# A fused attention and expert kernel: the attention tile's TensorE work regrouped into scores, values and transposes

## The chip, the cores and the metric

The kernel runs on one core of a Trainium2 chip. The metric is the device time of one execution in microseconds (us); the kernel before takes 827.62 us (median of three runs, 827.51 to 828.70). TensorE is called PE in the rows, its weight loads PEld, VectorE DVE, ScalarE ACT, GpSimd POOL, SyncE SP.

## The reference

Local attention with a few global keys, then four experts with fixed shares, then a gated product:

```
scores = scale * q @ k.T  - slope[h] * dist         # 2 batches, 8 heads, 768 positions, 64 wide
keep   = key < 8  or  0 <= q_pos - k_pos < 96       # all else is masked
a      = exp(scores - max);  a = a / (sum(a) + 1e-9)
x      = (a @ v)                                    # 1536 tokens x 512
out    = sum_e p[:, e] * (relu(x @ w1[e]) @ w2[e])  # 4 experts, 512 -> 1024 -> 512
final  = (((out @ wa) * (out @ wb)) @ w3) @ w_out
```

## The kernel before

The attention stage takes the first tenth of the time. It goes over twelve tiles of 128 queries. The first tile of each batch has only its own 128 keys; the ten others see a window of 232 keys (96 before, 8 global, 128 own). A tile has eight heads in two groups of four.

For a tile the work runs through five engines:

- TensorE: `scores` (line 246, eight matmuls into four PSUM tiles `sp`), `transposes` of the weights (line 284, four PSUM tiles `tp`, two for each group of heads; each holds two heads, and I call it a quarter of the tile), `values` (lines 325 and 326, into the PSUM tile `op`).
- VectorE: `least` for each head (line 261: bias, and the running minimum that becomes the exponent's offset), `inverse_sums` for each group (lines 231 and 232), the copy of one `tp` of each group to SBUF (line 291), and the low part of x, `xl` (line 468).
- ScalarE: `weights` for each head (line 272: the exponential with its sum; I number them 1 to 8 in a tile), the copy of the other `tp` of each group (line 291), the high part of x, `xh` (line 462), and from the seventh tile on a cast of a piece of an expert weight (line 343).
- GpSimd: `normalize` for each head (line 300), and the low part of the weight piece (line 344).

A later stage reads x as a high and a low part, hence two passes over each `op`.

The order on every engine is written out by hand: the loop over tiles (from line 357) emits the calls, and each engine executes its own in that order. An engine that waits for one instruction holds up all that stand behind it. Each loop step works on three tiles at once: scores of its own tile `u`, transposes of the tile one back, values of the tiles one and two back. TensorE's order in a step is: scores of u; transposes of group 0 of one back; values of group 1 of two back and of group 0 of one back; transposes of group 1 of one back. So four groups of matmuls follow each other in a step. PSUM has eight banks, four for `sp`, two for `tp` (`ps_t`), two for `op` (`ps_o`).

At the head of a step VectorE has the high cast of half an `op` and one copy, then two `least`; `inverse_sums` of the tile before comes after those. After the loop come the last tile's remaining steps, mixed with three expert products that are taken ahead (`experts.up_ahead`, lines 56 to 58); then the experts and the gate fill the rest, with matmuls of 128x512 almost without a gap.

Of the kernel before, what the change touches and what calls it, by code (L numbers as in the profile page):

```python
# [8 lines left out]
F32 = mybir.dt.float32  # L9
# [7 lines left out]
PSUM = bass.MemoryType.PSUM  # L17

P = 128
# [5 lines left out]
WIN = LW + GW + P  # L25
N, DM, E, F = B * S, H * D, 4, 1024
NPAIR = H // 2
KC, FC = DM // P, F // P
# [89 lines left out]
def banded_attention(tc, g, x_hi, x_lo, slots, experts):  # L118
    nc = tc.nc
    with ExitStack() as ctx:  # L120
# [5 lines left out]


        ps_s = ctx.enter_context(tc.tile_pool(name="ps_s", bufs=4, space=PSUM))
        ps_t = ctx.enter_context(tc.tile_pool(name="ps_t", bufs=2, space=PSUM))
        ps_o = ctx.enter_context(tc.tile_pool(name="ps_o", bufs=2, space=PSUM))  # L130
        mk = ctx.enter_context(tc.tile_pool(name="mk", bufs=1))
        two = ctx.enter_context(tc.tile_pool(name="at2", bufs=2))
        three_ = ctx.enter_context(tc.tile_pool(name="at3", bufs=3))
# [89 lines left out]
        later_bias(nc.gpsimd, (0, 1))  # L223

        st = {}
        raws, banks, firsts = [], [], {(order[-2], 1), (order[-1], 1)}

        def inverse_sums(u, gr):
            hs = slice(4 * gr, 4 * gr + 4)
            r, sums = st[u]["r"][:, hs], st[u]["sums"][:, hs]  # L230
            nc.vector.scalar_tensor_tensor(r, sums, 1e-9, sums, op0=ALU.add, op1=ALU.max)
            nc.vector.reciprocal(r, r)  # L232
# [21 lines left out]
        def least(u, gr, hh):  # L254

            w = WIN if u % NQ else P
            h = 4 * gr + hh
            t = three_.tile([P, WIN], F32, name="t", bufs=4)
            bb = bias[:, h] if u % NQ else bias0[:, h]
            nm = g.negmax[:, u * H + h : u * H + h + 1]  # L260
            nc.vector.tensor_tensor_reduce(  # L261
                out=t[:, 0:w], in0=st[u]["sp", gr][hh % 2][:, hh // 2, 0:w], in1=bb, scale=-SCALE,
                scalar=3.0e38, op0=ALU.add, op1=ALU.min, accum_out=nm,
            )
            st[u]["t", h] = t, nm

        def weights(u, gr, hh):

            w = WIN if u % NQ else P
            h = 4 * gr + hh  # L270
            t, nm = st[u].pop(("t", h))
            nc.scalar.activation(  # L272
                st[u][gr][:, hh, 0:w], t[:, 0:w], AF.Exp, bias=nm, scale=-1.0, accum_out=st[u]["sums"][:, h : h + 1]
            )

        def transposes(u, gr):
            pt = st[u][gr]
            tps = []
            for half in range(2):
                tp = ps_t.tile([P, 2, 2, P], F32, name="tp")  # L280
                for hh in range(2):
                    for j in range(2 if u % NQ else 1):
                        c = slice(j * (LW + GW), j * (LW + GW) + P)
                        nc.tensor.transpose(tp[:, hh, j], pt[:, 2 * half + hh, c], g.ident)  # L284
                tps.append(tp)
            st[u][gr] = tps

        def copy(u, gr, half):
            nj = 2 if u % NQ else 1
            sb = two.tile([P, 2, 2, P], F32, name="ptT", bufs=4)  # L290
            (nc.scalar.copy if half else nc.vector.tensor_copy)(sb[:, :, 0:nj], st[u][gr][half][:, :, 0:nj])
            st[u][gr][half] = sb
# [17 lines left out]
        def values(u, gr):  # L310

            i = u % NQ
            va, vo = values_of[u]
            if (u, gr) in firsts:
                banks.append((ps_o.tile([P, 4, P], F32, name="op"), []))
            o = banks[-1][0][:, 2 * len(banks[-1][1]) :][:, 0:2]
            banks[-1][1].append((u, gr))
            st[u]["o", gr] = o
            for hh in range(4):
                h, ab = 4 * gr + hh, hh % 2  # L320
                sb = st[u][gr][hh // 2]
                os_ = o[ab * D : (ab + 1) * D, hh // 2]
                vs = slice(h * D, (h + 1) * D)
                if i:
                    nc.tensor.matmul(os_, va[:, vs], sb[0 : LW + GW, ab, 0], start=True, stop=False)  # L325
                    nc.tensor.matmul(os_, vo[:, vs], sb[:, ab, 1], start=False, stop=True)  # L326
                else:
                    nc.tensor.matmul(os_, vo[:, vs], sb[:, ab, 0], start=True, stop=True)

        def outputs(u, gr):  # L330
            return st[u]["o", gr], x_hi, x_lo, u, slice(2 * gr, 2 * gr + 2)


        def load_weight(f):

# [7 lines left out]
            nc.scalar.copy(hi, raw)  # L343
            return lambda: nc.gpsimd.tensor_tensor(lo, raw, hi.bitcast(F32), op=ALU.subtract)

        def high(steps, copy=None):
            for step in steps:
                split_x_hi(nc, *outputs(*step), copy)

        def low(steps):  # L350
            for step in steps:
                split_x_lo(nc, *outputs(*step))

        nt = len(order)
        first = second = []
        for m, u in enumerate(order):
            one_back, two_back = (order[m - k] if m >= k else None for k in (1, 2))
            if 0 <= m - W_TILE < 4:
                load_weight(m - W_TILE)
            if m + 2 < nt:  # L360
                fetch(order[m + 2])
            if m + 1 < nt:
                fetch_v(order[m + 1])
            scores(u, 0)
            scores(u, 1)
            if m < len(FILL):
                keep_warm(FILL[m])
            high(second, nc.vector.tensor_copy)
            if m >= 2:
                for half in range(2):  # L370
                    copy(two_back, 1, half)
            n = m - W_TILE - 2
            rest = piece(n // 2, n % 2 * 256, n % 2 * 256 + 256) if n >= 0 else None
            for hh in range(2):
                least(u, 0, hh)
                weights(u, 0, hh)
            if m:
                inverse_sums(one_back, 1)
                transposes(one_back, 0)
                copy(one_back, 0, 1)  # L380
            least(u, 0, 2)
            weights(u, 0, 2)
            if m == 0:
                first_bias(1)
            least(u, 1, 0)
            least(u, 0, 3)
            weights(u, 0, 3)
            weights(u, 1, 0)
            if m:
                copy(one_back, 0, 0)  # L390
                normalize(one_back, 1, range(4))
            if m == 1:
                later_bias(nc.scalar, (5,))
            least(u, 1, 1)
            weights(u, 1, 1)
            inverse_sums(u, 0)
            least(u, 1, 2)
            weights(u, 1, 2)
            gone = first, second
            first, second = [(two_back, 1)] if m >= 2 else [], [(one_back, 0)] if m else []  # L400
            firsts.update((first + second)[0:1])
            for step in first + second:
                values(*step)
            high(first)
            low(gone[0])
            least(u, 1, 3)
            weights(u, 1, 3)
            low(gone[1])
            if m == 0:
                later_bias(nc.vector, (2, 3))  # L410
            if m == 1:
                later_bias(nc.scalar, (6, 7))
                later_bias(nc.vector, (4,))
            normalize(u, 0, range(4))
            if rest:
                rest()
            if m:
                transposes(one_back, 1)
        last, prior = order[-1], order[-2]
        out = experts.up_ahead(ps_s)  # L420
        for half in range(2):
            copy(prior, 1, half)
        high(second)
        inverse_sums(last, 1)
        normalize(last, 1, range(3))
        normalize_last(last, 1)
        transposes(last, 0)
        for half in range(2):
            copy(last, 0, half)
        low(first + second)  # L430
        values(prior, 1)
        out()
        high([(prior, 1)])
        low([(prior, 1)])
        transposes(last, 1)
        for half in range(2):
            copy(last, 1, half)
        out = experts.up_ahead(ps_s)
        for f in range(3):
            piece(f, F // 2, F)()  # L440
        values(last, 0)
        values(last, 1)
        out()
        out = experts.up_ahead(ps_s)
        high([(last, 0), (last, 1)])
        low([(last, 0), (last, 1)])
        split(nc, *slots[3], raws[3])
        out()

# [10 lines left out]
def split_x_hi(nc, tp, x_hi, x_lo, u, ks, copy=None):  # L460
    c, j = divmod(u, TPC)
    (copy or nc.scalar.copy)(x_hi[c][:, ks, j * P : (j + 1) * P], tp)


def split_x_lo(nc, tp, x_hi, x_lo, u, ks):
    c, j = divmod(u, TPC)
    sl = slice(j * P, (j + 1) * P)
    nc.vector.tensor_tensor(x_lo[c][:, ks, sl], tp, x_hi[c][:, ks, sl].bitcast(F32), op=ALU.subtract)
# [847 lines left out]
```

## Time and profile before

| | us |
|---|---|
| median of three runs | 827.62 |
| the profiled execution | 827.62 |
| its span on the chip | 825.7 |
| TensorE busy | 814.3 |
| VectorE busy | 509.9 |
| GpSimd busy | 315.6 |
| ScalarE busy | 283.5 |

The time outside the span is 1.9 us. A row of the timeline has the start, the duration, the engine and line, what is written and read, how many instructions the row merges, and in brackets how long the engine was idle before and what it waited for. The matmul rows of scores, transposes and values count two passes for each 4-byte matmul of scores and values. A step from the start of one row to the start of the next on the same engine is the time that the engine really gives to the first; durations overlap a little.

### The profile page before, as it was taken

The numbers are of one execution on the slowest core, as the hardware profiler recorded it, in microseconds if no ns is written. First come the engines' busy times: TensorE is split into PE (matmuls) and PEld (weight loads), VectorE is DVE, ScalarE is ACT, GpSimd is POOL, SyncE is SP. The second block draws the span as 40 slices with busy tenths as digits, with TensorE's granted clock in tenths as the row PEclk, the third lists the DMA queues.
The fourth block names the chain that finished last, engine by engine and source line by source line (L and its number), as shares of the span: only waits on it lengthen the run. The fifth ranks groups of instructions, "written<-read, shape, count | busy, mean of one in ns | idle before, by whom it ended". The sixth has DMA issues, their size and how long they took to land.

```text
span 825.7 us, 11047 instructions
## 1 busy us (share of the span) xinstructions
PE 814.3 (99%) x4003; PEld 669.5 (81%) x4003; DVE 509.9 (62%) x967; ACT 283.5 (34%) x595; POOL 315.6 (38%) x318
## 2 busy tenths in 40 slices
PE   8999999999999999999999999999999999999997
PEld 5888888888888888888888888888788888888875
DVE  7997446557755557778648573665543743887850
ACT  6997221223321213333324321332542432333210
POOL 6787023534356554641243341422370003333300
PEclk9999999999999999999999999999999999999999
DMA  8950333558453547743101102111523210201011
GB/s 252 274 152 2 104 129 119 154 161 250 158 166 107 152 150 231 228 153 102 39 25 52 39 26 64 52 64 43 189 88 101 78 52 26 102 26 52 0 52 55
DMA packets 38133, 88.11 MB, mean 107 GB/s; under 512 B 3690, under 2 KB 9882, under 8 KB 38070
## 3 DMA queue, kind: packets, MB, share of 16 engines
q1 hardware_dynamic: 37398, 86.79, 33.2%
q8 instruction: 33, 0.54, 0.3%
q10 hardware_dynamic: 672, 0.54, 0.3%
q14 instruction: 30, 0.25, 0.1%
HBM read 73.66 MB, written 13.66 MB: 106 GB/s over the span
## 4 chain that ended last, share of the span: by engine, by line
PE 96%; DVE 1%; ACT 1%; DMA 1%; issue 0%; DVEq 0%; ACTq 0%
PE z L56 18%; PE z L58 18%; PE z L57 18%; PE o L58 11%; PE o L56 11%; PE o L57 11%; PE tp L284 2%; PE sp L246 2%; PE op L325 2%; PE op L326 1%; ACT pt L272 1%; DMA keys<-in_k_dram 1%; PE sp L56 0%; PE sp L58 0%; PE sp L57 0%
## 5 line engine op out<-in xcount | busy, mean ns | idle before, releaser
L58 PE MATMUL z<-xh,sl 128*128 128x512 f32 x428 | 166.6, 389 | 0.0
L56 PE MATMUL z<-xh,sh 128*128 128x512 f32 x428 | 166.5, 389 | 0.0
L57 PE MATMUL z<-xl,sh 128*128 128x512 f32 x428 | 166.5, 389 | 0.0
L565 POOL TENSOR_TENSOR cr<-cr,cb 128x512 f32<-128x512 f32 x40 | 51.6, 1290 | 126.6 <-issue 118.8
L58 PEld LDWEIGHTS z<-xh,sl 128*128 128x128 f32 x428 | 80.3, 188 | 17.0 <-DVE sl L51 0.2
L57 PEld LDWEIGHTS z<-xl,sh 128*128 128x128 f32 x428 | 80.4, 188 | 16.8
L56 PEld LDWEIGHTS z<-xh,sh 128*128 128x128 f32 x428 | 80.3, 188 | 16.5
L51 POOL TENSOR_TENSOR sl<-wr,sh 128x512 fp32r<-128x512 f32 (+1 forms) x32 | 32.1, 1023 | 149.5 <-ACT sh L50 149.5
L51 DVE TENSOR_TENSOR sl<-wr,sh 128x1024 fp32r<-128x1024 f32 (+1 forms) x57 | 70.4, 1241 | 23.5 <-ACT sh L50 22.8
L819 POOL TENSOR_TENSOR acc<-acc,t 128x512 f32<-128x512 f32 x36 | 49.2, 1399 | 84.8 <-DVE t L818 84.8
L50 ACT CAST sh<-wr 128x1024 fp32r<-128x1024 f32 (+2 forms) x89 | 70.5, 815 | 21.4 <-PE z L57 10.3
L550 POOL TENSOR_SCALAR ca<-ca 128x512 f32<-128x512 f32 x40 | 61.8, 1545 | 26.8 <-ACT ca L548 26.8
L718 DVE TENSOR_TENSOR t<-t,z 128x512 f32<-128x512 f32 x56 | 37.4, 680 | 31.9 <-PE z L58 27.4
L300 POOL TENSOR_TENSOR pt<-pt,r 128x232 f32<-128x232 f32 (+1 forms) x95 | 48.8, 545 | 14.6 <-DVE r L232 5.2
L56 PE MATMUL z<-sh,sh 128*128 128x512 f32 x128 | 49.9, 390 | 0.8 <-DVE t L818 0.8
L58 PE MATMUL z<-sh,sl 128*128 128x512 f32 x128 | 49.8, 389 | 0.0
L57 PE MATMUL z<-sl,sh 128*128 128x512 f32 x128 | 49.8, 389 | 0.0
L272 ACT ACTIVATE pt<-t,negmax 128x232 f32<-128x232 f32 (+1 forms) x96 | 44.5, 466 | 7.3 <-DVE negmax L261 7.1
L51 POOL TENSOR_TENSOR sl<-t,sh 128x256 fp32r<-128x256 f32 (+1 forms) x24 | 23.0, 973 | 31.2 <-ACT sh L50 31.0
L261 DVE CUSTOM_DVE_ANT_0 t<-sp,bias 128x232 f32<-128x232 f32 (+1 forms) x96 | 32.4, 368 | 0.8 <-PE sp L246 0.8
L56 PE MATMUL o<-h0h,sh 128*128 128x512 f32 x84 | 32.8, 390 | 0.0
L57 PE MATMUL o<-h0l,sh 128*128 128x512 f32 x84 | 32.7, 389 | 0.0
(256 smaller groups left out, 1733.9 us busy)
## 6 DMA issues: line engine op xcount, KB each, us to landing
wr<-in_w_moe_dram SPq DMA_DIRECT2D x44, 512.0 KB, 3.4
raw<-in_w3t_dram SPq DMA_DIRECT2D x16, 512.0 KB, 4.1
raw<-in_w_ab_dram SPq DMA_DIRECT2D x16, 512.0 KB, 4.4
wr<-wab_d SPq DMA_DIRECT2D x16, 512.0 KB, 3.2
raw<-in_w_out_dram SPq DMA_DIRECT2D x8, 512.0 KB, 3.4
w3t_d<-cr SPq DMA_DIRECT2D x16, 256.0 KB, 2.5
wab_d<-cr SPq DMA_DIRECT2D x16, 256.0 KB, 2.2
wr<-w3t_d SPq DMA_DIRECT2D x8, 512.0 KB, 3.3
```

Of the source, the lines that this page charges most:

```text
L50: nc.scalar.copy(hi, src)
L51: (lo_engine or nc.vector).tensor_tensor(lo, src, hi.bitcast(F32), op=ALU.subtract)
L56: nc.tensor.matmul(out, wh, xh, start=start, stop=False)
L57: nc.tensor.matmul(out, wh, xl, start=False, stop=False)
L58: nc.tensor.matmul(out, wl, xh, start=False, stop=stop)
L261: nc.vector.tensor_tensor_reduce(out=t[:, 0:w], in0=st[u]["sp", gr][hh % 2][:, hh // 2, 0:w], in1=bb, scale=-SCALE, scalar=3.0e38, op0=ALU ...
L272: nc.scalar.activation(st[u][gr][:, hh, 0:w], t[:, 0:w], AF.Exp, bias=nm, scale=-1.0, accum_out=st[u]["sums"][:, h : h + 1])
L300: nc.gpsimd.tensor_tensor(pt[:, hh, 0:w], pt[:, hh, 0:w], r[:, hh : hh + 1].to_broadcast([P, w]), op=ALU.mult)
L550: nc.gpsimd.tensor_scalar(a, a, 2.0**-15, None, op0=ALU.max)
L565: nc.gpsimd.tensor_tensor(rest, rest, top.bitcast(F32), op=ALU.add)
L718: add = lambda o, a, b: nc.vector.tensor_tensor(o, a, b, op=ALU.add)
L819: nc.gpsimd.tensor_tensor(acc[c][:, d], acc[c][:, d], t, op=ALU.add)
```

## The change

In each loop step TensorE now does three groups: scores of both head groups of `u`, values of both head groups of the tile two back, transposes of both head groups of the tile one back. A tile's `op` is written in one go into one bank (`ps_o` has one buffer), `ps_t` gets three buffers, and `t`, the tile between `least` and `weights`, six in place of four. The x casts go over the whole `op` (128x512): high on ScalarE, low on VectorE; the high cast of half an `op` on VectorE is gone. `inverse_sums` and `normalize` of the tile before's second group move to the head of the step.

```diff
-        ps_t = ctx.enter_context(tc.tile_pool(name="ps_t", bufs=2, space=PSUM))
-        ps_o = ctx.enter_context(tc.tile_pool(name="ps_o", bufs=2, space=PSUM))
+        ps_t = ctx.enter_context(tc.tile_pool(name="ps_t", bufs=3, space=PSUM))
+        ps_o = ctx.enter_context(tc.tile_pool(name="ps_o", bufs=1, space=PSUM))
...
-            high(second, nc.vector.tensor_copy)
+            if m:
+                inverse_sums(one_back, 1)
+                normalize(one_back, 1, range(4))
             if m >= 2:
                 for half in range(2):
                     copy(two_back, 1, half)
...
-            for hh in range(2):
+            for hh in range(4):
                 least(u, 0, hh)
                 weights(u, 0, hh)
-            if m:
-                inverse_sums(one_back, 1)
-                transposes(one_back, 0)
-                copy(one_back, 0, 1)
...
             least(u, 1, 1)
+            least(u, 1, 2)
+            inverse_sums(u, 0)
+            if m >= 2:
+                values(two_back, 0)
+                values(two_back, 1)
+                split_x_hi(nc, *outputs(two_back))
             weights(u, 1, 1)
-            inverse_sums(u, 0)
-            least(u, 1, 2)
+            if m:
+                transposes(one_back, 0)
+                for half in (1, 0):
+                    copy(one_back, 0, half)
             weights(u, 1, 2)
-            for step in first + second:
-                values(*step)
-            high(first)
-            low(gone[0])
             least(u, 1, 3)
             weights(u, 1, 3)
-            low(gone[1])
+            if m >= 2:
+                split_x_lo(nc, *outputs(two_back))
...
             if m:
                 transposes(one_back, 1)
...
+        for gr in range(2):
+            values(prior, gr)
         out()
+        for gr in range(2):
+            transposes(last, gr)
```

VectorE at the head of a loop step, before: `xh` is the high part of x, `ptT` the transposed weights, `t` and `negmax` come from `least`, `r` and `sums` belong to the tile before.

```order
L462 CAST xh0_70<-op_586 128x2x128 [waits Activation_49]
L291 COPY ptT_649<-tp_613 128x512 [waits PE_49]
L261 ISA t_653,negmax_69<-sp_632,bias_97 128x232 [waits PE_49]
L261 ISA negmax_69 128x1
L261 ISA t_656,negmax_69<-sp_633,bias_97 128x232 [waits PE_49]
L261 ISA negmax_69 128x1
L231 SCALAR_TENSOR_TENSOR r_529<-sums_528 128x4 [waits Activation_49]
L232 RECIPROCAL r_529<-r_529 128x4 [waits DVE_49]
```

VectorE at the same place after the change:

```order
L449 TENSOR_TENSOR xl0_73<-op_557,xh0_70 128x4x128 [waits Activation_49]
L231 SCALAR_TENSOR_TENSOR r_517<-sums_516 128x4 [waits Activation_49]
L232 RECIPROCAL r_517<-r_517 128x4 [waits DVE_49]
L291 COPY ptT_640<-tp_599 128x512 [waits PE_49]
L261 ISA t_644,negmax_69<-sp_618,bias_97 128x232 [waits PE_49]
L261 ISA negmax_69 128x1
```

The row that waits for ScalarE's sums of the tile before stood behind a cast, a copy and two `least`; now it stands in front of the copy and of all `least`.

ScalarE over one loop step late in the stage, before:

```order
L291 COPY ptT<-tp 128x512
L343 CAST sh_80<-wr 128x256
L272 ACTIVATE pt,sums<-t,negmax 128x232 x2
L291 COPY ptT<-tp 128x512
L272 ACTIVATE pt,sums<-t,negmax 128x232 x5
L462 CAST xh_72<-op 128x2x128
L272 ACTIVATE pt,sums<-t,negmax 128x232
```

ScalarE over the same step after the change:

```order
L291 COPY ptT<-tp 128x512
L340 CAST sh_80<-wr 128x256
L272 ACTIVATE pt,sums<-t,negmax 128x232 x5
L443 CAST xh_72<-op 128x4x128
L272 ACTIVATE pt,sums<-t,negmax 128x232
L291 COPY ptT<-tp 128x512
L272 ACTIVATE pt,sums<-t,negmax 128x232 x2
```

The copy of the first group's `tp` moved from behind exponential 2 to behind exponential 6; the cast covers 512 columns in place of 256 and stands behind exponential 5 in place of 7.

TensorE, the second half of the transposes and the next tile's scores after the change:

```order
L284 MATMUL tp_599<-ident_63,pt_425 128x128 [waits Pool_49]
L284 MATMUL tp_599<-ident_63,pt_425 128x128
L284 MATMUL tp_599<-ident_63,pt_425 128x128 [waits Pool_49]
L284 MATMUL tp_599<-ident_63,pt_425 128x128
L284 MATMUL tp_604<-ident_63,pt_425 128x128 [waits Activation_49,Pool_49]
L284 MATMUL tp_604<-ident_63,pt_425 128x128
L284 MATMUL tp_604<-ident_63,pt_425 128x128 [waits Pool_49]
L284 MATMUL tp_604<-ident_63,pt_425 128x128
L246 MATMUL sp_618<-keys_96,qr_403 128x232 [waits DMAHW2_49,DMAHW1_49,DVE_49]
```

TensorE, the transposes of the second group and the next scores before:

```order
L284 MATMUL tp_613<-ident_63,pt_431 128x128 [waits PE_49,Pool_49]
L284 MATMUL tp_613<-ident_63,pt_431 128x128
L284 MATMUL tp_613<-ident_63,pt_431 128x128 [waits Pool_49]
L284 MATMUL tp_613<-ident_63,pt_431 128x128
L284 MATMUL tp_618<-ident_63,pt_431 128x128 [waits Pool_49]
L284 MATMUL tp_618<-ident_63,pt_431 128x128
L284 MATMUL tp_618<-ident_63,pt_431 128x128 [waits Pool_49]
L284 MATMUL tp_618<-ident_63,pt_431 128x128
L246 MATMUL sp_632<-keys_96,qr_409 128x232 [waits DMAHW7_49,DMAHW6_49]
```

With three buffers and four `tp` in a row, the fourth waits for ScalarE, which has to copy the second of the same row out first.

## Rows read from the trace of the kernel before

**Rows 1.** The page's first part: busy time, share and instructions of each engine.

```profile
PE 814.3 (99%) x4003; PEld 669.5 (81%) x4003; DVE 509.9 (62%) x967; ACT 283.5 (34%) x595; POOL 315.6 (38%) x318
```

**Rows 2.** Stretches: length, busy PE, PEld, DVE, ACT, POOL, granted clock, DMA, GB/s.

```profile
18.00:24.00 6.00, 4.88 (x52) 3.79 (x50) 5.34 (x29) 5.54 (x23) 4.41 (x9) 1.00 0.89 259
60.60:66.60 6.00, 6.00 (x67) 5.15 (x68) 5.39 (x26) 5.50 (x22) 5.00 (x10) 1.00 0.12 41
```

**Rows 3.** Timeline of ScalarE: first exponential of the third, fifth and twelfth tile.

```profile
15.55 0.49 ACT L272 ACTIVATE pt<-t,negmax 128x232 f32<-128x232 f32 x1
...
26.47 0.49 ACT L272 ACTIVATE pt<-t,negmax 128x232 f32<-128x232 f32 x1 [0.59 <-DVE negmax L261]
...
68.15 0.49 ACT L272 ACTIVATE pt<-t,negmax 128x232 f32<-128x232 f32 x1 [0.20 <-DVE negmax L261]
```

**Rows 4.** Timeline of TensorE: one loop step without a wait.

```profile
59.56 1.09 PE L284 MATMUL tp<-ident,pt 128*128 128x128 f32 x8
60.59 1.84 PE L246 MATMUL sp<-keys,qr 64*128 64x232 f32 x16
62.35 1.09 PE L284 MATMUL tp<-ident,pt 128*128 128x128 f32 x8
63.38 0.45 PE L325 MATMUL op<-ptT,va 104*64 104x128 f32 x4
...
65.41 0.77 PE L284 MATMUL tp<-ident,pt 128*128 128x128 f32 x5
```

**Rows 5.** Timeline of the weight loads: the wait in the step before that.

```profile
58.48 0.20 PEld L325 LDWEIGHTS op<-ptT,va 104*64 104x64 f32 x4 [0.22 <-DVE ptT L291]
```

**Rows 6.** Timeline of ScalarE: exponentials, a cast of 256 columns, a copy of 512.

```profile
46.08 0.49 ACT L272 ACTIVATE pt<-t,negmax 128x232 f32<-128x232 f32 x1
...
46.57 0.48 ACT L272 ACTIVATE pt<-t,negmax 128x232 f32<-128x232 f32 x1
...
47.04 0.48 ACT L272 ACTIVATE pt<-t,negmax 128x232 f32<-128x232 f32 x1
...
48.46 0.35 ACT L462 CAST xh<-op 128x256 fp32r<-128x256 f32 x1
48.71 0.49 ACT L272 ACTIVATE pt<-t,negmax 128x232 f32<-128x232 f32 x1
...
49.19 0.56 ACT L291 COPY ptT<-tp 128x512 f32<-128x512 f32 x1
49.66 0.41 ACT L343 CAST sh<-wr 128x256 fp32r<-128x256 f32 x1
50.30 0.49 ACT L272 ACTIVATE pt<-t,negmax 128x232 f32<-128x232 f32 x1 [0.24 <-DVE negmax L261]
```

**Rows 7.** Timeline of VectorE: inverse sums that wait for exponential 4, a copy, a `least`.

```profile
47.24 0.16 DVE L231 SCALAR_TENSOR_TENSOR r<-sums 128x4 f32<-128x4 f32 x1 [0.36 <-ACT pt L272]
...
47.53 0.37 DVE L261 CUSTOM_DVE_ANT_0 t<-sp,bias 128x232 f32<-128x232 f32 x1
...
49.18 0.68 DVE L291 COPY ptT<-tp 128x512 f32<-128x512 f32 x1
49.80 0.40 DVE L261 CUSTOM_DVE_ANT_0 t<-sp,bias 128x232 f32<-128x232 f32 x1
```

**Rows 8.** Timeline: ScalarE's copies and the transposes that wait for one.

```profile
19.86 0.36 ACT L291 COPY ptT<-tp 128x256 f32<-128x256 f32 x1
...
20.36 1.07 PE L284 MATMUL tp<-ident,pt 128*128 128x128 f32 x8 [0.36 <-ACT ptT L291]
...
63.48 0.58 ACT L291 COPY ptT<-tp 128x512 f32<-128x512 f32 x1 [0.26 <-PE tp L284]
```

**Rows 9.** Timeline of TensorE behind the loop: first product ahead, transposes, second product.

```profile
72.28 0.48 PE L56 MATMUL sp<-xh,sh 128*128 128x512 f32 x1
...
77.18 1.09 PE L284 MATMUL tp<-ident,pt 128*128 128x128 f32 x8
78.03 0.48 PE L56 MATMUL sp<-xh,sh 128*128 128x512 f32 x1
```

More of the change, by code (lines that the diff above doesn't have):

```diff
@@ L225, in banded_attention @@
         st = {}
-        raws, banks, firsts = [], [], {(order[-2], 1), (order[-1], 1)}
+        raws = []
         def inverse_sums(u, gr):
@@ L257, in least @@
             h = 4 * gr + hh
-            t = three_.tile([P, WIN], F32, name="t", bufs=4)
+            t = three_.tile([P, WIN], F32, name="t", bufs=6)
             bb = bias[:, h] if u % NQ else bias0[:, h]
@@ L313, in values @@
             va, vo = values_of[u]
[L314 to L318, printed above, removed]
+            if gr == 0:
+                st[u]["o"] = ps_o.tile([P, 4, P], F32, name="op")
+            o = st[u]["o"][:, 2 * gr : 2 * gr + 2]
             for hh in range(4):
@@ L328, in values, with outputs @@
                     nc.tensor.matmul(os_, vo[:, vs], sb[:, ab, 0], start=True, stop=True)
-        def outputs(u, gr):
-            return st[u]["o", gr], x_hi, x_lo, u, slice(2 * gr, 2 * gr + 2)
+        def outputs(u):
+            return st[u]["o"], x_hi, x_lo, u, slice(0, KC)
         def load_weight(f):
@@ L344, in piece @@
             return lambda: nc.gpsimd.tensor_tensor(lo, raw, hi.bitcast(F32), op=ALU.subtract)
[L346 to L352, printed above, removed]
         nt = len(order)
-        first = second = []
         for m, u in enumerate(order):
@@ L373, in banded_attention @@
             rest = piece(n // 2, n % 2 * 256, n % 2 * 256 + 256) if n >= 0 else None
-            for hh in range(2):
+            for hh in range(4):
                 least(u, 0, hh)
                 weights(u, 0, hh)
-            if m:
-                inverse_sums(one_back, 1)
-                transposes(one_back, 0)
-                copy(one_back, 0, 1)
-            least(u, 0, 2)
-            weights(u, 0, 2)
             if m == 0:
                 first_bias(1)
[L385 to L391, printed above, removed]
             if m == 1:
                 later_bias(nc.scalar, (5,))
+            least(u, 1, 0)
+            weights(u, 1, 0)
             least(u, 1, 1)
+            least(u, 1, 2)
[4 more added lines that the diff above has]
+                split_x_hi(nc, *outputs(two_back))
             weights(u, 1, 1)
-            inverse_sums(u, 0)
-            least(u, 1, 2)
+            if m:
+                transposes(one_back, 0)
+                for half in (1, 0):
+                    copy(one_back, 0, half)
             weights(u, 1, 2)
-            gone = first, second
-            first, second = [(two_back, 1)] if m >= 2 else [], [(one_back, 0)] if m else []
-            firsts.update((first + second)[0:1])
-            for step in first + second:
-                values(*step)
-            high(first)
-            low(gone[0])
             least(u, 1, 3)
             weights(u, 1, 3)
-            low(gone[1])
+            if m >= 2:
+                split_x_lo(nc, *outputs(two_back))
             if m == 0:
@@ L420, in banded_attention @@
         out = experts.up_ahead(ps_s)
+        inverse_sums(last, 1)
+        normalize(last, 1, range(3))
         for half in range(2):
             copy(prior, 1, half)
-        high(second)
-        inverse_sums(last, 1)
-        normalize(last, 1, range(3))
         normalize_last(last, 1)
[L427 to L431, printed above, removed]
-        out()
[L433 to L437, printed above, removed]
+        for gr in range(2):
+            values(prior, gr)
+        out()
+        for gr in range(2):
+            transposes(last, gr)
+            if gr == 0:
+                split_x_hi(nc, *outputs(prior))
+            for half in range(2):
+                copy(last, gr, half)
+            if gr == 0:
+                split_x_lo(nc, *outputs(prior))
         out = experts.up_ahead(ps_s)
@@ L440, in banded_attention @@
             piece(f, F // 2, F)()
-        values(last, 0)
-        values(last, 1)
+        for gr in range(2):
+            values(last, gr)
         out()
         out = experts.up_ahead(ps_s)
-        high([(last, 0), (last, 1)])
-        low([(last, 0), (last, 1)])
+        split_x_hi(nc, *outputs(last))
+        split_x_lo(nc, *outputs(last))
         split(nc, *slots[3], raws[3])
```

## The prediction

> **What bounds the kernel now.** I read the page first, then the stretches of the attention stage, then the timelines of TensorE, ScalarE and VectorE there. TensorE is busy 814.3 of 825.7 us [rows 1], so what delays the attention stage delays the end: nothing behind it has slack to give back. In the steady part of the stage TensorE is busy all the time, but the others are close behind: of 6.00 us ScalarE works 5.50, VectorE 5.39, GpSimd 5.00 [rows 2]. So the order in which they hand work to each other counts as much as TensorE's own load.
>
> The period of a loop step: the first exponential of the fifth tile starts at 26.47, that of the twelfth at 68.15 [rows 3], so (68.15 - 26.47) / 7 = 5.95 us. A step in which TensorE waits for nothing lasts from 59.56 to 65.41, 5.85 us [rows 4]: transposes 1.03 (59.56 to 60.59), scores 1.76 (to 62.35), transposes 1.03 (to 63.38), both values 2.03 (to 65.41). Other steps have a wait of about 0.2 for a copy of VectorE in the middle of the values [rows 5]. TensorE is the bound, with 0.1 us a step lost.
>
> **The change part by part.**
>
> *TensorE's groups.* Four groups a step become three, with the same matmuls. What a change of group costs: eight transposes take 1.03 when values follow [rows 4], and 0.85 (77.18 to 78.03) when matmuls of the full 128x128 follow [rows 9], so 0.18. If TensorE stays the bound, a step shrinks from 5.85 to 5.67.
> The Trainium skill, TensorEngine Tiling (Array Packing), section Key Properties, says that a change of tiling mode drains TensorE, so fewer changes are a gain; the 0.18 agrees with that, and by that rule alone the time would fall (the third rival).
>
> *The ring of ScalarE and VectorE.* This is the term that decides. After the change VectorE starts a step with the inverse sums of the tile before, which wait for that tile's exponential 8, ScalarE's last work for that tile's weights. Behind them in VectorE's queue stand the copy of 512 columns and all `least` of the new tile, and exponential 1 of the new tile waits for the first `least`. So exponential 8 of one tile and exponential 1 of the next are tied by a chain that no other work fills, and between 1 and 8 ScalarE runs without a pause. Once round, with steps from start to start:
>
> - Exponential 8 to inverse sums: exponential at 46.57, inverse sums that waited for it at 47.24 [rows 6, 7]: 0.67.
> - Inverse sums to the next VectorE instruction: 47.24 to 47.53 [rows 7]: 0.29.
> - Copy to `least`: 49.18 to 49.80 [rows 7]: 0.62.
> - `least` to exponential 1: 49.80 to 50.30 [rows 6, 7]: 0.50.
> - Exponentials 1 to 5: the first after another kind of work takes 0.49 (46.08 to 46.57), the others 0.47 (46.57 to 47.04) [rows 6]: 0.49 + 4 x 0.47 = 2.37.
> - The high cast of 512 columns, which no row has on ScalarE: the nearest rows are the cast of 256 columns, 0.25 from start to start (48.46 to 48.71), and the copy of 512 columns out of PSUM, 0.47 (49.19 to 49.66), at most its whole 0.56 [rows 6]. I take 0.47, for the same width and the same source; the ends are 0.25 and 0.56.
> - Exponential 6: 48.71 to 49.19, 0.48. Copy of the first group's `tp`: 0.47. Exponential 7: 0.49 [rows 6].
>
> Sum: 0.67 + 0.29 + 0.62 + 0.50 + 2.37 + 0.47 + 0.48 + 0.47 + 0.49 = 6.36 us, with the ends of the cast 6.14 and 6.45. Before, the same wait stood behind a cast, a copy and two `least`, and exponentials 1 and 2 did not depend on it; the ring through it was far shorter than 5.95. The copy of the second group's `tp` and the cast of a weight piece cost nothing: ScalarE does them while it waits for exponential 1, 0.67 + 0.29 + 0.62 + 0.50 = 2.08 us after exponential 8, and needs 0.49 + 0.47 and at most 0.64 (49.66 to 50.30) for them, 1.60 [rows 6].
>
> *The fourth quarter of the transposes.* The order shows it waiting for ScalarE: its PSUM buffer is that of the second quarter, freed by the copy behind exponential 6. This closes a second ring, through TensorE: copy 0.56 [rows 6]; copy's end to transposes, 19.86 + 0.36 to 20.36, 0.14 [rows 8]; four transposes, half of 0.85, and a change of group, 0.43 + 0.18 = 0.61; scores 1.76; values 2.03 [rows 4]; start of the transposes to the copy of the second quarter, 62.35 to 63.48, 1.13 [rows 4, 8]. Sum 6.23. That is under 6.36, so this ring waits for the first one, but it too is above 5.95. So TensorE will stand still before the fourth quarter: its own work is 5.67, the step 6.36, about 0.7 idle a step.
>
> *VectorE and GpSimd.* VectorE loses one cast and gets one low pass of 512 columns for two of 256. That is a saving on an engine that will now wait between the low pass and the inverse sums, so I count nothing. GpSimd's first normalize starts earlier, with 2.2 us of work between inverse sums that lie about 3 us apart; nothing changes in its sum, and no gain is taken. Had GpSimd no such slack, it would be its 5.00 a step [rows 2] that counts, still under 6.36.
>
> *The ramp and the tail.* The third tile's first exponential I leave at 15.55 [rows 3]. The next step has copies of half the width, on ScalarE 0.25 as the cast of that width, on VectorE between 0.25 and 0.62, taken as 0.35: 6.36 - 0.22 - 0.27 = 5.87, to 21.42. Then 6.36 to the fifth tile, 27.78, and seven more to the twelfth: 27.78 + 7 x 6.36 = 72.30, against 68.15 before, 4.15 later.
> From there to the first product ahead: exponentials, cast, exponential 6 (2.37 + 0.47 + 0.48 = 3.32), the copy and the wait (0.56 + 0.14), four transposes (0.43): 4.45, at 76.75. Before, it was at 72.28 [rows 9]: 4.47 later. Behind it stood transposes, one group's values, transposes; now both groups' values and both transposes: one group's values more, 2.03 / 2 = 1.02 (moved out of the last step, where TensorE waits anyway), and about 0.1 for the fourth quarter, which now follows a VectorE copy. So the experts begin 4.47 + 1.02 + 0.1 = 5.6 us later.
>
> Sum: the profiled execution takes 827.62, which is also the median, with 1.9 us outside the span, untouched. 827.62 + 5.6 = 833.2 us.
>
> **The rivals.**
>
> *TensorE's ring binds, not ScalarE's.* If the hand-overs between ScalarE and VectorE are shorter than the rows say, or the cast costs 0.25, a step is 6.23. Nine steps of 0.13 less: 833.2 - 1.2 = 832.0. For it: the two sums differ by only 0.13. Against it: each step of the first ring is read from a row with the same wait.
>
> *It gets a little worse still.* If the inverse sums' two small instructions take longer beside GpSimd than the 0.29 of the row, or the ramp starts later, 0.2 a step over ten steps: 835.2. For it: GpSimd is busy in 5.00 of 6.00 [rows 2]. Against: the row has GpSimd's load already.
>
> *Faster: TensorE stays the bound and has a change of group less.* This needs a first ring under 5.67, so 0.7 of its terms would have to be wrong. Then (5.95 - 5.67) x 7 = 2.0 us less in the steady part, nothing in the ramp, where TensorE is busy only 4.88 of 6.00 [rows 2], and the tail is even: 825.6. For it: TensorE's share now, and VectorE's relief. Against: the order of VectorE's queue.
>
> *No change.* The gain from the groups is eaten by the wait of the fourth quarter, with a step of 5.95 as before: 827.6. It needs both rings 0.3 to 0.4 shorter than their rows.
>
> **How the numbers follow.** The forecast 0.55, TensorE's ring 0.17, the worse variant 0.16, faster 0.06, no change 0.06. What is no change is about 0.2%, 1.7 us, the least that a measurement can tell here. So slower 0.88, same 0.06, faster 0.06. The likeliest case is 833.2, with 832.0 to 834.0 from the ends of the cast's price: down it is 0.13 a step, where the second ring takes over, up 0.09, over nine steps. The range takes in the second ring below and the worse variant above: 830.8 to 836.0.
>
> **What would show it.** Right: first exponentials about 6.4 us apart from the fifth to the twelfth tile, the inverse sums at the head of a step waiting for exponential 8, exponential 1 waiting some 0.7 us for `least`, TensorE idle about 0.7 us a step before the fourth quarter of the transposes, with ScalarE's copy named, and the twelfth tile's first exponential near 72.3. TensorE's ring binds: ScalarE waits for TensorE's transposes before the copy behind exponential 6, and steps are 6.2. Faster: TensorE without a wait and steps of 5.7. The forecast is wrong if the inverse sums do not wait at the head of a step, or if the exponentials 1 to 8 do not run without a pause.

## The result and the profile after

The changed kernel takes 835.16 us (median of six runs, 834.84 to 836.19) against 827.57 us (827.29 to 828.70) before, beside it on the same chip: a ratio of 1.0091, with a 95% interval of 1.0078 to 1.0104. The profiled execution takes 834.85 us, its span is 832.9 us. The forecast was 833.2, between 830.8 and 836.0.

The first part of the page answers to [rows 1]: no engine has more work than before, TensorE's sum is the same to 0.3 us, and the span is 7.2 us longer. What came in is waiting.

```profile
PE 814.6 (98%) x4002; PEld 670.3 (80%) x4003; DVE 507.5 (61%) x945; ACT 285.2 (34%) x593; POOL 316.3 (38%) x318
```

The two stretches of [rows 2], in the same columns:

```profile
18.00:24.00 6.00, 5.28 (x56) 4.26 (x54) 4.58 (x25) 5.16 (x21) 4.34 (x8) 0.99 0.97 271
60.60:66.60 6.00, 5.09 (x61) 4.53 (x60) 4.74 (x23) 5.64 (x20) 4.54 (x9) 1.00 0.27 79
```

In the steady stretch TensorE works 5.09 of 6.00 us where it worked 6.00. The granted clock there is 1.00 of full speed (2.4 GHz) as before, so none of the loss in that stretch is the clock's.

In the ramp, the stretch before the fifth tile, it is not so. From 14.8 to 18.1 us the granted clock was 0.50 (1.2 GHz), where the kernel before has 1.00. In the timeline of TensorE of the changed kernel, it had stood still for 2.04 us up to 13.73, and the scores behind that took 2.81 us (14.07 to 16.88) for the 1.76 of full clock:

```profile
13.73 0.41 PE L284 MATMUL tp<-ident,pt 128*128 128x128 f32 x2 [2.04 <-POOL pt L300]
14.07 2.88 PE L246 MATMUL sp<-keys,qr 64*128 64x232 f32 x16
16.88 1.68 PE L326 MATMUL op<-ptT,vo 128*64 128x128 f32 x16
```

That fall cost the end little. Of the six executions, the one with a mean clock of 1.000 took 834.84 us, and the five with 0.996 or 0.997 took 834.85 to 836.19. And in a run below whose clock did not fall (`e5_swap_alone`) the fourth tile's first exponential starts at 21.98, against 22.00 here.

ScalarE's timeline of the changed kernel, the first exponential of the tiles from the fourth on, answers to [rows 3]:

```profile
22.00 0.49 ACT L272 ACTIVATE pt<-t,negmax 128x232 f32<-128x232 f32 x1 [0.72 <-DVE negmax L261]
28.25 0.49 ACT L272 ACTIVATE pt<-t,negmax 128x232 f32<-128x232 f32 x1 [0.90 <-DVE negmax L261]
...
40.74 0.49 ACT L272 ACTIVATE pt<-t,negmax 128x232 f32<-128x232 f32 x1 [0.59 <-DVE negmax L261]
47.46 0.49 ACT L272 ACTIVATE pt<-t,negmax 128x232 f32<-128x232 f32 x1 [1.08 <-DVE negmax L261]
54.19 0.49 ACT L272 ACTIVATE pt<-t,negmax 128x232 f32<-128x232 f32 x1 [1.09 <-DVE negmax L261]
...
74.38 0.49 ACT L272 ACTIVATE pt<-t,negmax 128x232 f32<-128x232 f32 x1 [1.08 <-DVE negmax L261]
```

There are two periods: 6.24 to 6.25 us up to 40.74, and from there five steps of 6.73, (74.38 - 40.74) / 5. The five longer steps are the tiles in which GpSimd has the low part of a weight piece. The twelfth tile begins at 74.38, against 68.15 before and 72.30 in the forecast.

One slow step, in the timeline of the changed kernel, of all engines:

```profile
58.22 0.63 PE L284 MATMUL tp<-ident,pt 128*128 128x128 f32 x4 [0.91 <-ACT ptT L291]
...
58.46 0.48 ACT L272 ACTIVATE pt<-t,negmax 128x232 f32<-128x232 f32 x1
...
58.97 0.74 POOL L341 TENSOR_TENSOR sl<-wr,sh 128x256 fp32r<-128x256 f32 x1
59.07 0.66 DVE L231 SCALAR_TENSOR_TENSOR r<-sums 128x4 f32<-128x4 f32 x1 [0.91 <-ACT pt L272]
...
59.85 0.66 DVE L291 COPY ptT<-tp 128x512 f32<-128x512 f32 x1
...
60.43 0.39 DVE L261 CUSTOM_DVE_ANT_0 t<-sp,bias 128x232 f32<-128x232 f32 x1
...
60.92 0.49 ACT L272 ACTIVATE pt<-t,negmax 128x232 f32<-128x232 f32 x1 [1.09 <-DVE negmax L261]
...
63.02 0.16 DVE L231 SCALAR_TENSOR_TENSOR r<-sums 128x4 f32<-128x4 f32 x1 [0.28 <-ACT pt L272]
...
63.30 0.57 ACT L443 CAST xh<-op 128x512 fp32r<-128x512 f32 x1
63.76 0.49 ACT L272 ACTIVATE pt<-t,negmax 128x232 f32<-128x232 f32 x1
64.24 0.57 ACT L291 COPY ptT<-tp 128x512 f32<-128x512 f32 x1
64.71 0.49 ACT L272 ACTIVATE pt<-t,negmax 128x232 f32<-128x232 f32 x1
64.96 0.63 PE L284 MATMUL tp<-ident,pt 128*128 128x128 f32 x4 [0.91 <-ACT ptT L291]
65.19 0.48 ACT L272 ACTIVATE pt<-t,negmax 128x232 f32<-128x232 f32 x1
```

This is the ring that the prediction described, link by link: exponential 8 at 58.46, inverse sums that wait for it at 59.07, copy, `least`, exponential 1 at 60.92, and ScalarE without a pause to the next exponential 8 at 65.19, 6.73 later. TensorE stands still 0.91 us before the fourth quarter; in the three steps of 6.24 it is 0.42. The new thing is the row at 59.07. The same instruction takes 0.16 at 63.02; here it takes 0.66, and it ends at 59.73, with GpSimd's row at 58.97, which ends at 59.71.

The waits of the changed kernel from 29 to 79 us (total, times, longest) name the same chain; before, TensorE had only waits of some 0.2 [rows 5]:

```profile
DVE r L231 <- ACT pt L272: 7.4, 15, 0.9
ACT pt L272 <- DVE negmax L261: 6.9, 7, 1.1
PE tp L284 <- ACT ptT L291: 5.8, 8, 0.9
```

TensorE behind the loop, in the timeline of the changed kernel, for [rows 9]: the first rows of the three products ahead.

```profile
78.80 0.48 PE L56 MATMUL sp<-xh,sh 128*128 128x512 f32 x1
...
85.59 0.48 PE L56 MATMUL sp<-xh,sh 128*128 128x512 f32 x1
...
90.47 0.51 PE L56 MATMUL sp<-xh,sh 128*128 128x512 f32 x1
```

The third began at 82.92 in the kernel before:

```profile
82.92 0.51 PE L56 MATMUL sp<-xh,sh 128*128 128x512 f32 x1
```

So it is 7.55 us later, and from here on the two kernels do the same to 0.4 us: the loss of 7.2 (profiled executions) to 7.6 us (medians) is in the attention stage.

### The profile page after: what moved, and what is told of

It is laid out like the page before. It is cut to its first block, busy times and chain, and to the rows that moved or that the text cites. A ratio compares the mean times of both kernels' runs of the same rounds, so it can differ in the third digit from the quotient of the medians.

```text
span 832.9 us, 11020 instructions
## 1 busy us (share of the span) xinstructions
PE 814.6 (98%) x4002; PEld 670.3 (80%) x4003; DVE 507.5 (61%) x945; ACT 285.2 (34%) x593; POOL 316.3 (38%) x318
## 4 chain that ended last, share of the span: by engine, by line
PE 89%; ACT 6%; DVE 2%; issue 1%; DMA 1%; POOL 0%; ACTq 0%; DVEq 0%; POOLq 0%
PE z L56 18%; PE z L57 18%; PE z L58 18%; PE o L58 11%; PE o L56 11%; PE o L57 11%; ACT pt L272 5%; DVE ptT L291 1%; ACT xh L443 1%; DMA keys<-in_k_dram 1%; DVE r L231 1%; ACT ptT L291 1%; PE sp L246 0%; PE tp L284 0%; DVE t L261 0%
## 5 line engine op out<-in xcount | busy, mean ns | idle before, releaser
L51 DVE TENSOR_TENSOR sl<-wr,sh 128x1024 fp32r<-128x1024 f32 (+1 forms) x57 | 69.9, 1233 | 23.6 <-ACT sh L50 22.9
L284 PE MATMUL tp<-ident,pt 128*128 128x128 f32 x176 | 24.4, 279 | 9.9 <-ACT ptT L291 7.8
```

The lines of the kernel that those rows point to most:

```text
L51: (lo_engine or nc.vector).tensor_tensor(lo, src, hi.bitcast(F32), op=ALU.subtract)
```

## The experiments

Theory A is that of the prediction: the step is set by the ring through ScalarE and VectorE, closed by the inverse sums at the head of the tile. The rivals changed from run to run.

**The inverse sums back behind the second `least`** (`e1_sums_later`), all else as changed:

```diff
-            if m:
-                inverse_sums(one_back, 1)
-                normalize(one_back, 1, range(4))
...
             for hh in range(4):
                 least(u, 0, hh)
                 weights(u, 0, hh)
+                if m and hh == 1:
+                    inverse_sums(one_back, 1)
+                    normalize(one_back, 1, range(4))
```

> The changed kernel with the inverse sums and the normalize of the tile before's second group moved back from the head of the step to behind the second least; all else as changed. Theory A (the ring exponential 8 - inverse sums - copy - least - exponential 1 sets the step): the ring is cut, steps fall from 6.25 and 6.73 us to the ring through TensorE's fourth quarter, about 6.15 in both halves of the stage, and the kernel to 835.2 - 3 x 0.1 - 5 x 0.58 = 832.0 us (831.2 to 832.8). Rival B (the wait of the fourth quarter of the transposes for ScalarE's copy, 7.8 us in the trace, is the cause): that wait is untouched, so steps stay at 6.2 and 6.7 and the time at 835.

Measured: 831.54 us, ratio 1.0055 (1.0038 to 1.0071), all steps 6.18. As A has it. The first ring is open, both losses that it brought are gone (0.06 in the steps of 6.24, 0.55 in those of 6.73), and a ring through the fourth quarter holds the loop. The steps give 3 x 0.06 + 5 x 0.55 = 2.9 of the 3.6 us; the rest lies in the ramp, where the fourth tile's first exponential starts at 20.67 in place of 22.00. This run's timeline of ScalarE, TensorE and VectorE shows the ring:

```profile
60.59 0.48 ACT L272 ACTIVATE pt<-t,negmax 128x232 f32<-128x232 f32 x1
61.08 0.56 ACT L291 COPY ptT<-tp 128x512 f32<-128x512 f32 x1
...
61.78 0.63 PE L284 MATMUL tp<-ident,pt 128*128 128x128 f32 x4 [0.36 <-POOL pt L300]
...
62.34 1.84 PE L246 MATMUL sp<-keys,qr 64*128 64x232 f32 x16
...
63.42 0.40 DVE L261 CUSTOM_DVE_ANT_0 t<-sp,bias 128x232 f32<-128x232 f32 x1 [0.63 <-PE sp L246]
...
63.93 0.49 ACT L272 ACTIVATE pt<-t,negmax 128x232 f32<-128x232 f32 x1 [0.54 <-DVE negmax L261]
```

ScalarE's copy ends at 61.64 and the fourth quarter starts 0.14 later (the row names GpSimd, but its last `normalize` had ended long before); then come the scores, `least`, exponential 1, and ScalarE's queue up to the next copy: 0.70 + 0.56 + 1.08 + 0.51 + 3.33 = 6.18. This is not the prediction's second ring, which went on from the scores over the values and the next transposes to ScalarE's copy. Here that copy waits for no transposes: it starts as soon as exponential 6 is done.

**GpSimd's low part of the piece ahead of its four `normalize`** (`e2_piece_low_earlier`), to move it out from under the inverse sums:

```diff
-            normalize(u, 0, range(4))
             if rest:
                 rest()
+            normalize(u, 0, range(4))
```

> The changed kernel with GpSimd's low part of the weight piece moved ahead of the normalize of the tile's own first group, so that it no longer runs at the head of the next step. Theory A' (in the steps with a piece the inverse sums take 0.66 us in place of 0.16 because GpSimd's low part runs at that moment): all steps are 6.25, 5 x 0.48 = 2.4 us less, 832.8 us (832.0 to 833.6). Rival (ScalarE's cast of the piece, 0.41 us, is what lengthens those steps from 6.25 to 6.73): the cast is still there at the same place, so no change, 835.

Measured: 832.61 us, ratio 1.0065 (1.0048 to 1.0082), all steps from the fourth tile on 6.24 to 6.25. The inverse sums' row of this run, at the place of the row at 59.07:

```profile
59.25 0.16 DVE L231 SCALAR_TENSOR_TENSOR r<-sums 128x4 f32<-128x4 f32 x1 [0.50 <-ACT pt L272]
```

So the slow steps were slow by that overlap, and by nothing else: 5 x 0.49 = 2.45 us, and the medians differ by 835.16 - 832.61 = 2.55. The profiled execution, 833.83, shows less of it, since here the fall of the clock to 0.50 came later in the ramp (20.5 to 23.6), and the step from the third to the fourth tile took 6.76 us in place of 5.95.

**What holds the inverse sums.** Two runs kept place and order, and changed only the instruction: in `e7_sums_one_input` it reads the sums once, as a tensor_scalar; in `e8_sums_by_reduce` it is a tensor_reduce over one element, without the 1e-9.

```diff
-            nc.vector.scalar_tensor_tensor(r, sums, 1e-9, sums, op0=ALU.add, op1=ALU.max)
+            nc.vector.tensor_scalar(r, sums, 1e-9, None, op0=ALU.add)
```

```diff
-            nc.vector.scalar_tensor_tensor(r, sums, 1e-9, sums, op0=ALU.add, op1=ALU.max)
+            nc.vector.tensor_reduce(r, sums.unsqueeze(2), op=ALU.max, axis=mybir.AxisListType.X)
```

> The changed kernel, with one instruction of the inverse sums altered: the scalar_tensor_tensor of 128x4 that reads the sums twice becomes a tensor_scalar that reads them once (sums + 1e-9). Place and order stay. In the changed kernel the first takes 0.66 us in place of 0.16 wherever GpSimd's low part of a weight piece runs. Theory L (VectorE is held because its instruction reads SBUF twice, and GpSimd reads SBUF at that time): it takes about 0.16, steps with a weight piece 6.24 like the others, 835.2 - 5 x 0.49 = 832.7 us (832.0 to 833.3). Rival M (any small VectorE instruction on SBUF is held there, whatever it reads): it stays at 0.6 to 0.7, steps of 6.73, 835 us. The Trainium skill, SBUF - State Buffer, section Who interferes with whom, states L, and adds that a tensor_scalar may use both ports in a faster mode and then be held too, which would look like M here; the run beside this one has an instruction that it says is never held.

> The changed kernel, with the first instruction of the inverse sums as a tensor_reduce over one element (it reads the sums once and leaves out the 1e-9). Theory L: it is not held beside GpSimd and takes some 0.2 us, steps of 6.2 to 6.3 throughout, 832.7 us (832.0 to 833.5). Rival M: held like any other, 0.6 to 0.7, steps of 6.7 with a weight piece, 835 us. If this one is free and the tensor_scalar is held, the held thing is a second read port, not the second input. The Trainium skill, SBUF - State Buffer, section Who interferes with whom, states that a tensor_reduce is never held on this chip.

Measured: 835.05 us for the tensor_scalar (ratio 1.0095, 1.0078 to 1.0111), 832.59 for the tensor_reduce (1.0059, 1.0042 to 1.0076). The timeline of GpSimd and VectorE with the tensor_scalar:

```profile
58.93 0.73 POOL L341 TENSOR_TENSOR sl<-wr,sh 128x256 fp32r<-128x256 f32 x1
59.02 0.66 DVE L231 TENSOR_SCALAR r<-sums 128x4 f32<-128x4 f32 x1 [0.90 <-ACT pt L272]
```

And with the tensor_reduce:

```profile
59.03 0.73 POOL L341 TENSOR_TENSOR sl<-wr,sh 128x256 fp32r<-128x256 f32 x1
59.15 0.16 DVE L231 TENSOR_REDUCE r<-sums 128x4 f32<-128x4 f32 x1 [0.49 <-ACT pt L272]
```

The same 128x4 sums, under the same GpSimd instruction: one is held until GpSimd ends, the other is not. Theory L as I had put it (two inputs) does not cover the tensor_scalar, and rival M (any small instruction) fails by the tensor_reduce. The Trainium skill, SBUF - State Buffer, section Who interferes with whom, covers all three: VectorE shares its second pair of SBUF ports with GpSimd, whoever starts first keeps it for its whole instruction, a VectorE instruction with two SBUF inputs contends for it with a GpSimd instruction that reads SBUF, a tensor_scalar or copy may take it for a faster mode, a tensor_reduce never does on this chip. The three durations, 0.66, 0.66 and 0.16, agree with that; which port it was no trace shows, and all three have GpSimd starting first.

**The fourth quarter on VectorE's copy** (`e5_swap_alone`): with this order the first quarter, whose PSUM buffer the fourth then takes, is copied first.

```diff
-                for half in (1, 0):
+                for half in (0, 1):
                     copy(one_back, 0, half)
```

> The changed kernel, with nothing else altered than the order in which the copies of the first two quarters are emitted, (0, 1) in place of (1, 0), so that the fourth quarter's transposes wait for VectorE's copy in place of ScalarE's; the inverse sums stay at the head of the tile. Theory A (the loop is set by the ring exponential 8, inverse sums, least, exponential 1, ScalarE's queue, exponential 8, which this edit does not touch): steps stay at 6.2 us before the weight pieces and 6.7 with them, 834 to 836 us. Rival B (what was gained in the run that had both edits, 5.2 us over the run that had the sums moved alone, was the fourth quarter's wait by itself, whatever the sums do): 835.2 - 5.2 = 830.0 us, steps about 6.3 with the pieces.

Measured: 834.00 us, ratio 1.0075 (1.0060 to 1.0091); steps 6.23 and 6.72. As A has it: with the second ring opened and the first left, nothing changes in the period. TensorE still waits, now with VectorE's name on it, so the wait before the fourth quarter is a follower of the first ring here. In this run's timeline:

```profile
57.30 0.63 PE L284 MATMUL tp<-ident,pt 128*128 128x128 f32 x4 [0.89 <-DVE ptT L291]
...
64.02 0.63 PE L284 MATMUL tp<-ident,pt 128*128 128x128 f32 x4 [0.89 <-DVE ptT L291]
```

What it does win, 1.2 us by the medians and 0.9 by the profiled executions, is not in ScalarE's steps: the fourth tile's first exponential starts at 21.98 for 22.00, the twelfth's at 74.26 for 74.38. It is in TensorE's place within the step. VectorE's copy of the first quarter ends earlier than ScalarE's of the second, so the fourth quarter comes earlier in each step (the fourth tile's scores behind it start at 19.42 in place of 20.42), and at the end of the loop that lead is left over. In this run's timeline the first product ahead, which stands behind the last fourth quarter, starts 0.95 us before the 78.80 of the changed kernel:

```profile
77.85 0.48 PE L56 MATMUL sp<-xh,sh 128*128 128x512 f32 x1
```

**Both edits together** (`e3_sums_later_swap`, and once more as `e6_later_swap_again`): the diffs of e1 and e5.

> As the first of these, and the copies of the first group's two quarters are emitted in the other order, so that the fourth quarter's PSUM buffer is freed by VectorE's copy of the first quarter and not by ScalarE's copy of the second. Theory A with the second ring: the ring through TensorE is now start of transposes to VectorE's copy 0.70, copy 0.66, wait 0.1, last quarter 0.56, scores 1.77, values 1.97: 5.8 us a step, eight steps of 0.35 less than in the first: 829.2 us (828.2 to 830.4), with the wait for the fourth quarter nearly gone. Rival (the order of the copies does not matter, since VectorE reaches its copy later than ScalarE does): 832 as the first.

> The kernel with both edits (inverse sums moved behind the second least, copies in the order (0, 1)) once more, for its place against the kernel before: 326 hundredths over 823, that is 826.3 us (825.8 to 826.9), a ratio of 0.9985 (0.998 to 0.999) with steps of 5.82 us against 5.9. Theory A gives a gain, since TensorE waits only some 0.2 us a step for VectorE's copy of the first quarter, where the kernel before pays more changes between kinds of matmul. Rival: the gain in the earlier run was the spread of the runs, and the ratio's interval takes in 1.

Measured: 826.32 us, ratio 0.9988 (0.9979 to 0.9998), and the second time 827.07, 0.9990 (0.9981 to 1.0000). Steps of 5.82, against 5.95 before. This is 2.9 and 2.1 us under the first expectation and below its range; its sum left out that the ramp gains too (the fifth tile's first exponential starts at 24.53, against 26.85 in e1). With the kernels before that were measured beside them, the four cases are: neither edit +7.6 us, the inverse sums moved alone +4.2 (e1), the copies swapped alone +6.4 (e5), both edits -1.0 and -0.5. TensorE's timeline, second run, over one step:

```profile
57.88 1.84 PE L246 MATMUL sp<-keys,qr 64*128 64x232 f32 x16
...
59.64 0.45 PE L323 MATMUL op<-ptT,va 104*64 104x128 f32 x4
...
61.61 2.16 PE L284 MATMUL tp<-ident,pt 128*128 128x128 f32 x16
63.70 1.84 PE L246 MATMUL sp<-keys,qr 64*128 64x232 f32 x16
```

TensorE is the bound again: scores 1.76, values 1.97, transposes 2.09, where two groups of them would take 0.85 + 1.03 = 1.88 [rows 4, 9], so about 0.2 of waiting is left. The three groups by themselves are worth little. The twelfth tile's first exponential starts at 65.28, 2.9 us earlier than before, but 1.9 of that is won before the fifth tile and 0.9 in the seven steps behind it, and the group of values more in the tail takes 1.1 back. So the third product starts at 81.10, 1.8 us earlier than before, and the medians show 0.5 to 1.0 us of that, about what such runs can tell from nothing: the second interval reaches 1. In the first run's profiled execution (third product at 81.01, span 823.6 for 825.7) all of it reaches the end. In the second's (span 824.9) one wait of TensorE for VectorE, between 500 and 600 us, lasted 1.6 us where the kernel before has 0.8 and the first run 0.7; why it did is open. It is the fastest of the kernels tried, and hardly faster than the kernel before.

**Four groups, whole-tile casts** (`e4_four_groups_whole`): the kernel before with both values of the tile two back in one `op` and casts of 512 columns (six `ptT` buffers).

```diff
-            for step in first + second:
-                values(*step)
-            high(first)
-            low(gone[0])
+            if m >= 2:
+                values(two_back, 0)
+                values(two_back, 1)
+                split_x_hi(nc, *outputs(two_back))
...
-            low(gone[1])
+            if m >= 2:
+                split_x_lo(nc, *outputs(two_back))
```

> The kernel before with one part of the change alone: both values of the tile two back in one op, and whole-tile x casts (high on ScalarE, low on VectorE), but still four groups of matmuls a step, two transposes of four quarters on two PSUM buffers and the inverse sums behind two least. Theory A: no new ring, TensorE bound at 5.85 to 5.95 us a step, 0.1 less for the wait in the values, but one group's values (1.0 us) moves from the ramp, where TensorE idles, to the tail, where it does not: 827.6 - 0.8 + 1.0 = 827.8 us (827.0 to 828.8). Rival (the whole-tile cast on ScalarE, 0.47 for 0.25, makes ScalarE the bound): steps over 6.1 and 829 or more.

Measured: 830.45 us, ratio 1.0037 (1.0023 to 1.0052), steps 6.19: A's number was wrong here, since I had looked for the loss in the inverse sums alone. The rival's numbers came, its cause did not: ScalarE still stands idle 0.47 us a step before exponential 1. The timeline of ScalarE and VectorE shows a third ring of the same make:

```profile
50.37 0.56 ACT L447 CAST xh<-op 128x512 fp32r<-128x512 f32 x1
...
50.97 0.69 DVE L453 TENSOR_TENSOR xl<-op,xh 128x512 fp32r<-128x512 f32 x1 [0.80 <-ACT xh L447]
...
51.58 0.68 DVE L291 COPY ptT<-tp 128x512 f32<-128x512 f32 x1
...
52.17 0.39 DVE L261 CUSTOM_DVE_ANT_0 t<-sp,bias 128x232 f32<-128x232 f32 x1
...
52.67 0.49 ACT L272 ACTIVATE pt<-t,negmax 128x232 f32<-128x232 f32 x1 [0.47 <-POOL sl L342]
...
56.57 0.56 ACT L447 CAST xh<-op 128x512 fp32r<-128x512 f32 x1
```

The high cast stands late on ScalarE, the low pass that waits for it stands at the head of VectorE's next step, in front of the copy and of all `least`: 0.60 + 0.61 + 0.59 + 0.50 + 3.90 = 6.20. The row of exponential 1 names GpSimd's low part of a piece, which ends at 52.59, just behind `least` (52.56); the steps without a piece, 21.81 to 28.00 to 34.19, are as long, and their rows name `least`. This ring is read from the timeline; no run opened it.

## Why the prediction was right, and where it was short

*The bound.* Right. The forecast's mechanism, its wait and its place are in the profile after, with TensorE idle at the fourth quarter (0.42 us in the steps of 6.24 and 0.91 in those of 6.73, for about 0.7), and e1 takes the first ring away while e2, e5 and e8 leave it.

*The ring's sum.* Forecast 6.36. Without the hold it is 6.24: exponential 8 to inverse sums 0.61 for 0.67, copy to `least` 0.58 for 0.62, the rest within 0.02. The cast, the term without a row, was 0.46 for 0.47.

*The term that was mis-sized.* "Inverse sums to the next VectorE instruction: 0.29 [rows 7]." In the five steps with a weight piece it is 0.78 (59.07 to 59.85). The row at 47.24 was taken where GpSimd was just going idle, and so the sentence on the second rival, that "the row has GpSimd's load already", was wrong. The trace of the kernel before had the other case as well: in the steady part at 44.54, where the instruction took 0.27 us and ended at 44.81, with GpSimd's low part at 44.80, and most clearly in the tail:

```profile
72.04 1.64 POOL L300 TENSOR_TENSOR pt<-pt,r 128x232 f32<-128x232 f32 x3
...
73.13 0.56 DVE L231 SCALAR_TENSOR_TENSOR r<-sums 128x4 f32<-128x4 f32 x1
```

There the same instruction took 0.56 and ended at 73.69, with GpSimd's at 73.68. I take it that it cost nothing before, since no ring as long as a step ran through it; no run tests that.

*The ramp and the tail.* The third tile's first exponential, left at 15.55, came at 16.05, behind the 2.04 us in which TensorE stood still; the step behind it took 5.95 for 5.87. From the twelfth tile to the first product ahead: 4.42 for 4.45; from the first to the third product 1.03 longer than before, for 1.02 + 0.1.

Summed: forecast +5.6; ramp +0.5 + 0.08; three steps of 6.24 for 6.36, -0.34; five of 6.73, +1.84; product and tail -0.12. Together +7.55, the start of the third product. The case that came is in effect the second rival, inverse sums slower beside GpSimd, at 835.2, though by 0.37 in five steps and not 0.2 in ten, and with the later start of the ramp that it names too. The ends given for the likeliest case alone, 832.0 to 834.0, miss the time; the range holds it because its upper end was set for that rival.

*TensorE's ring.* That the fourth quarter, waiting for ScalarE's copy, closes a second ring just below the first is right, and so is that part of the loss stays while it is closed: e1 has steps of 6.18. But the ring that binds in e1 runs over `least`, exponential 1 and ScalarE's queue. The forecast's, over the values and the next transposes, adds up to 0.70 + 0.56 + 1.77 + 1.97 + 1.13 = 6.13 with e1's rows and the prediction's last term, so that 6.23 comes so near to 6.18 is in part luck. *Faster* and *no change* needed both rings shorter; e3 and e6, which open both, come near to them, with 0.5 to 1.0 us gained where *faster* had 2.0. That rival took the ramp and the tail as even; in e6 the ramp won 1.9 us and the tail lost 1.1, and the seven steps gave 0.9, not 2.0.

## What to carry to other kernels

When work moves to the head of a queue, look for the ring that it closes: add the hand-overs from one step's last result to the next step's first, over all engines, and compare the sum with the period; no engine's busy share shows it. A duration from one row is the duration beside what the other engines did at that moment: read the same instruction at all its places and take the slowest into the range. Opening one of two rings of like length gains only the difference, so both have to be opened before the bound goes back to the engine with the most work.

## What was not expected of the hardware

A VectorE instruction on 512 numbers, of 0.16 us, lasts 0.66 us when a GpSimd instruction of 0.74 us that reads SBUF has started 0.1 us before it, and ends together with it. That holds with two SBUF inputs and with a tensor_scalar of one; a tensor_reduce of the same numbers took 0.16 under the same load.
